# Loading the first-layer MLP weights in three DMAs of 112, 8 and 8 partitions instead of one of 128

## The chip, the cores and the metric

One core of one Trainium2 chip runs the whole program. The metric is device time in microseconds (us), lower is better. Executions of one kernel in one set of rounds agree within some 0.3%. Each kernel is compared with runs of the kernel before that were taken in the same rounds on the same chip.

## The reference, cut to what matters

A decode step of attention over a cached K and V, plus an MLP, added to a residual. The caches (8 x 32 heads x 4096 keys x 128, bf16, 268 MB each) are nearly all of the bytes. The MLP matters here only through its weights `w1`, 640 x 1728 bf16, 2.2 MB of 552 MB.

```python
xn = _layernorm(x)                                     # x: 8 x 1 x 640
out = x + attention(xn, k_cache, v_cache, wq, wo) + mlp(xn, w1, b1, w2, b2)
# mlp: h = gelu(layernorm(xn) @ w1 + b1);  h @ w2 + b2
```

## The kernel before: the parts that matter

All large loads go out from the sync engine (SP) on one DMA queue, in a fixed order: K tile 0, `wq`, K tile 1, `w1`, `w2` (two pieces), then V and K tiles in turn, 4 MB each, until the end. A tile's buffer is reused once it has been consumed; two K and two V buffers keep the queue filled.

```python
def ld(pos, dst, src, W, sem, R=()):          # a DMA from SP; W: what it writes, R: what it waits for
    add("sp", pos, lambda e: e.dma_start(dst, src() if callable(src) else src), R=R, W=W, sem=sem)
...
w1_sb = arena[:, o1:o2].rearrange("p (c f) -> p c f", c=DC)      # 128 partitions x 17280 bytes
...
ld(-95.2, w1_sb, B_w1.rearrange("(k c) f -> k c f", c=DC), ["w1"], "w1")
ld(-95.1, w2_sb[:, 0:FC, :], B_w2[0:FC * P, :].rearrange("(k c) n -> k c n", c=FC), ["w2"], "w2")
ld(-95.0, w2_sb[0:FR, FC, :], B_w2[FC * P:F, :], ["w2r"], "w2r")
...
add("pe", 1.0, pe_hidden, R=["w1", "xT1", "b1", "onesb", "zeros"], W=[it_h, "w1free"], X=[it_h])
```

Partition k of `w1_sb` gets five neighbouring rows of `w1`, one contiguous run of 17280 bytes. I call one partition's contiguous piece of a DMA a *run*; in the trace it is one DMA packet. Every load of 16 engines has added 16 to its semaphore, one step per engine, when all of them are done (W1: 16 steps, from 39.42 to 41.15 us). I call each of these steps a *landing*.

## Time and profile before

| | before |
|---|---|
| median, first set of runs | 1290.24 us (4 runs, 1289.99 to 1290.49) |
| profiled span | 1288.2 us |
| DMA rate over the span | 429 GB/s |
| VectorE busy | 1141.1 us, 89% |
| W1 runs (128 of 17280 bytes) | mean 0.648 us, median 0.644 |
| W2 runs (128 of 16640 bytes) | mean 0.628 us, median 0.620 |
| last K tile: mean / last of its 16 landings | 1252.46 / 1253.76 us |

The first fence has lines of the page of the kernel before: DMA busy share (in tenths) and GB/s in 40 slices of 32.2 us, then the load queue's packets, MB and share of 16 engines.

```profile
DMA  9999999999999999999999999999999999999998
GB/s 408 423 427 429 437 429 432 429 429 433 431 431 432 432 428 434 429 433 429 431 431 432 430 428 436 429 433 429 430 432 432 430 435 429 428 434 430 432 430 351
...
q1 hardware_dynamic: 21440, 551.80, 99.8%
```

Next, the chain of waits of the kernel before (start us, us, what). From 247 us until the short tail at the end it is only V-cache loads and the matmuls that consume them. With the queue at 99.8% throughout, what the DMA engines lose early can be expected to arrive at the end.

```profile
1.22 23.81 DMA KV_sb<-in_A_wq_dram
...
56.79 28.81 DMA KV_sb<-in_A_k_cache_dram
...
247.41 34.57 DMA KV_sb<-in_A_v_cache_dram
...
1228.27 35.19 DMA KV_sb<-in_A_v_cache_dram
1263.50 3.62 PE PV_ps L630 x32
1267.14 15.92 DMA KV_sb<-in_A_v_cache_dram
```

The third view is a table by stretch: start and end, length, each engine's busy us and instructions, granted clock, DMA share, GB/s. Most of W1 and all of W2 travel in these 13 us, at 421 and 415 GB/s.

```profile
core 0: us, PE busy (x) PEld busy (x) DVE busy (x) ACT busy (x) POOL busy (x), PEclk, DMA share, GB/s
35.00:41.00 6.00, 5.32 (x76) 4.34 (x77) 5.97 (x3) 3.96 (x8) 0.00 (x0) 1.00 0.99 421
41.00:48.00 7.00, 4.51 (x83) 3.96 (x82) 6.96 (x3) 5.84 (x11) 0.00 (x0) 0.69 1.03 415
```

### The profile page before, as it was taken

To read this page: it belongs to the slowest core of one execution; us is meant where nothing else is said; L and a number is where in the kernel's file an instruction comes from. 1 tells how busy PE (TensorE), PEld (TensorE's weight loads), DVE (VectorE), ACT (ScalarE), POOL (GpSimd) and SP (SyncE) were. 2 spreads that over 40 slices of the span, in tenths; PEclk is the share of its full clock that TensorE was granted. 3 is DMA by queue.
4 is the path that set the end of the run, shared out by engine and by line. 5 is a ranking of instruction groups with operands and counts; after the bars stand their busy time and mean duration, and the time that the engine had idled before them with its cause. 6 is when DMAs were issued, how large, how long until landed. Compare 5 with 4: busy or idle time off the path is not lost.

```text
span 1288.2 us, 19951 instructions
## 1 busy us (share of the span) xinstructions
PE 641.0 (50%) x7931; PEld 403.3 (31%) x7934; DVE 1141.1 (89%) x680; ACT 496.9 (39%) x1243; POOL 0.2 (0%) x4
## 2 busy tenths in 40 slices
PE   2754454444554455454455444544544554455456
PEld 1433233223333233232233232332332332333332
DVE  4989999998898898898988988988989989889895
ACT  1444344334344234343243342443432443433432
POOL 0000000000000000000000000000000000000000
PEclk9755555565555655656656556555565556655556
DMA  9999999999999999999999999999999999999998
GB/s 408 423 427 429 437 429 432 429 429 433 431 431 432 432 428 434 429 433 429 431 431 432 430 428 436 429 433 429 430 432 432 430 435 429 428 434 430 432 430 351
DMA packets 21488, 552.00 MB, mean 429 GB/s; under 512 B 2313, under 2 KB 2401, under 8 KB 4450
## 3 DMA queue, kind: packets, MB, share of 16 engines
q1 hardware_dynamic: 21440, 551.80, 99.8%
q8 instruction: 8, 0.13, 0.0%
q14 instruction: 6, 0.05, 0.0%
q10 hardware_dynamic: 34, 0.02, 0.0%
HBM read 551.80 MB, written 0.01 MB: 428 GB/s over the span
## 4 chain that ended last, share of the span: by engine, by line
DMA 77%; DVE 11%; PE 8%; issue 4%; ACT 0%; SPq 0%; DVEq 0%
DMA KV_sb<-in_A_v_cache_dram 73%; PE PV_ps L630 7%; DVE Y_sb L558 6%; DVE Y_sb L562 3%; DMA KV_sb<-in_A_k_cache_dram 2%; DVE S_sb L565 2%; DMA KV_sb<-in_A_wq_dram 2%; DVE oTn_sb L679 0%; DVE M_sb L577 0%; PE CH_ps L579 0%; SPq L372 0%; DVE rinv_sb L611 0%; PE PV_ps L640 0%; PE TR_ps L691 0%; PE TR_ps L470 0%
## 5 line engine op out<-in xcount | busy, mean ns | idle before, releaser
L558 DVE TENSOR_TENSOR Y_sb<-KV_sb,qbc_sb 128x6144 bf16<-128x6144 bf16 x128 | 429.0, 3352 | 67.0 <-DMA KV_sb<-in_A_k_cache_dram 51.8
L565 DVE TENSOR_REDUCE S_sb<-Y_sb 128x48 f32<-128x3072 bf16 x128 | 429.2, 3353 | 4.4
L529 ACT ACTIVATE KT_sb<-TR_ps 128x1024 bf16<-128x1024 bf16 x256 | 254.6, 1021 | 232.5 <-PE TR_ps L526 231.1
L630 PE MATMUL PV_ps<-KV_sb,P_sb 128*16 128x512 bf16 x2040 | 222.0, 609 | 132.0 <-DMA KV_sb<-in_A_v_cache_dram 132.0
L526 PE MATMUL TR_ps<-ident_bf,KV_sb 128*128 128x128 bf16 x2048 | 248.3, 308 | 53.1 <-DMA KV_sb<-in_A_k_cache_dram 52.6
L562 DVE TENSOR_TENSOR Y_sb<-Y_sb 128x3072 bf16<-128x3072 bf16 x128 | 225.0, 1758 | 4.4
L526 PEld LDWEIGHTS TR_ps<-ident_bf,KV_sb 128*128 128x128 bf16 x2048 | 200.4, 141 | 63.3 <-DMA KV_sb<-in_A_k_cache_dram 57.5
L536 PE MATMUL S_ps<-qk_sb,KT_sb 128*128 128x4 bf16 x2048 | 98.0, 170 | 140.3 <-ACT KT_sb L529 138.3
L649 ACT ACTIVATE E_sb<-PV_ps 128x512 bf16<-128x512 f32 (+1 forms) x65 | 38.5, 592 | 308.2 <-PE PV_ps L630 306.2
L536 PEld LDWEIGHTS S_ps<-qk_sb,KT_sb 128*128 128x128 bf16 x2048 | 85.9, 109 | 171.7 <-ACT KT_sb L529 171.7
L630 PEld LDWEIGHTS PV_ps<-KV_sb,P_sb 128*16 128x16 bf16 x2040 | 60.7, 120 | 246.3 <-DMA KV_sb<-in_A_v_cache_dram 137.2
L597 ACT ACTIVATE P_sb<-S_sb,NB_sb 32x128 bf16<-32x128 f32 x256 | 101.9, 398 | 3.8
L655 PE MATMUL C_ps<-sel_bf,E_sb 128*128 128x4 bf16 x256 | 16.9, 172 | 159.7 <-DVE rinv_sb L611 133.7
L591 ACT ACTIVATE NB_sb<-CH_ps 128x2 f32<-128x2 f32 (+1 forms) x33 | 5.7, 172 | 177.1 <-PE CH_ps L587 177.1
L579 PE MATMUL CH_ps<-ident_f,M_sb 128*2 128x128 f32 (+1 forms) x33 | 12.2, 369 | 117.7 <-DVE M_sb L577 117.7
L655 PEld LDWEIGHTS C_ps<-sel_bf,E_sb 128*128 128x128 bf16 x256 | 11.4, 103 | 189.4 <-DVE rinv_sb L611 136.4
L546 ACT ACTIVATE S_sb<-S_ps 32x32 f32<-32x32 f32 x256 | 48.2, 188 | 32.0 <-PE S_ps L536 29.8
L597 ACT ACTIVATION_READ_ACCUMULATOR P_sb<-S_sb,NB_sb 32x1 f32 x256 | 47.1, 184 | 0.0
L579 PEld LDWEIGHTS CH_ps<-ident_f,M_sb 128*2 128x2 f32 (+1 forms) x33 | 2.6, 80 | 120.6 <-DVE M_sb L577 120.6
L673 DVE MEMSET oTn_sb<- 128x16 uint32 x30 | 2.2, 72 | 31.1 <-PE ACC_ps L704 31.1
L581 DVE TENSOR_REDUCE M_sb<-CH_ps 2x4 f32<-2x128 f32 (+1 forms) x33 | 9.2, 279 | 15.9 <-PE CH_ps L579 15.9
L704 PE MATMUL ACC_ps<-oTn_sb,wo_sb 128*128 128x8 bf16 x600 | 20.8, 169 | 0.0
(96 smaller groups left out, 212.8 us busy)
## 6 DMA issues: line engine op xcount, KB each, us to landing
KV_sb<-in_A_k_cache_dram SPq DMA_DIRECT2D x64, 4096.0 KB, 26.8
KV_sb<-in_A_v_cache_dram SPq DMA_DIRECT2D x63, 4096.0 KB, 35.2
KV_sb<-in_A_wq_dram SPq DMA_DIRECT2D x1, 5120.0 KB, 23.8
wo_sb<-in_A_wo_dram SPq DMA_DIRECT2D x7, 640.0 KB, 30.8
KV_sb<-in_B_w_dram SPq DMA_DIRECT2D x1, 2160.0 KB, 39.0
w_sb<-in_B_w_dram SPq DMA_DIRECT2D x1, 2080.0 KB, 43.8
KV_sb<-in_A_v_cache_dram SPq DMA_DIRECT2D x1, 2048.0 KB, 12.7
KV_sb<-in_A_v_cache_dram SPq DMA_DIRECT2D x2, 1024.0 KB, 15.1
```

What stands on the lines that cost most here:

```text
L526: r = e.transpose(TR_ps[:, it.box[0], jj * P:(jj + 1) * P], kv[:, n * BK + jj, :], ident_bf[:, :])
L529: add("act", t - 0.59 + 0.12 * n, lambda e: e.activation(KT_sb[:, m % NS, :, :].rearrange("p a b -> p (a b)"), TR_ps[:, it.box[0], :], ACT ...
L536: r = e.matmul(S_ps[:, c:c + HT], KT_sb[:, m % NS, jj, :], qk_sb[:, :, i], start=True, stop=True)
L546: r = e.activation(S_sb[s, g % SR, i, 0:JP], S_ps[s, 0:JP * HT].rearrange("p (j a) -> p j a", a=HT)[:, :, a], ACT.Copy)
L558: return e.tensor_tensor(y, kv[:, j0:j1, :], qbc_sb[:, g % 2, i, :][:, None, :].to_broadcast([P, nj, P]), ALU.mult)
L562: lambda e, y=y, y2=y2: e.tensor_tensor(y2, y[:, :, 0:P // 2], y[:, :, P // 2:P], ALU.add),
L565: lambda e, y2=y2, j0=j0, j1=j1: e.tensor_reduce(S_sb[:, g % SR, i, j0:j1], y2, AX.X, ALU.add),
L597: r = e.activation(P_sb[s, i, :, a, :], S_sb[s, g % SR, i, :].rearrange("p (m c) -> p m c", c=4), ACT.Exp, bias=NB_sb[s, g % 2, i:i + 1], ...
L630: r = e.matmul(PV_ps[32 * ct:32 * ct + HT * 4, t % 2, :], P_sb[:, i, m, :, :].rearrange("p a c -> p (a c)"), vv[:, 4 * m:4 * m + 4, :, :], ...
L649: add("act", pos, lambda e: e.activation(E_sb[:, k, 0:n], PV_ps[:, k, 0:n], ACT.Copy), R=[("PV", k)] + ["wo"] * (t % GT and not last), W=[ ...
L655: r = e.matmul(OT_i, E_sb[:, t % 2, c * P:(c + 1) * P], sel_bf[:, c:HT * 4:4], start=(c == 0), stop=(c == 3 and not last))
L704: r = e.matmul(ACC_ps[:, c * B:(c + 1) * B], wo_sb[:, a, c * P:(c + 1) * P], oTn_sb[:, a, :], start=False, stop=False, skip_group_check=True)
```

## The change

The intent: both DMAs of 8 partitions go to the same eight of the 16 DMA engines, which I call the *first eight* (no trace numbers the engines). With 112 + 8 + 8 partitions, the first eight move 7 + 1 + 1 = 9 runs of W1 and the other eight move 7. If the first eight were ahead of the others, the field (how far the sixteen engines lie apart in time) would be evened out.

```diff
-        ld(-95.2, w1_sb, B_w1.rearrange("(k c) f -> k c f", c=DC), ["w1"], "w1")
+        w1v = B_w1.rearrange("(k c) f -> k c f", c=DC)
+        for n, (p0, p1) in enumerate(((0, P - 16), (P - 16, P - 8), (P - 8, P))):
+            ld(-95.2 + 0.01 * n, w1_sb[p0:p1], w1v[p0:p1], ["w1_%d" % n], "w1")
...
-        add("pe", 1.0, pe_hidden, R=["w1", "xT1", "b1", "onesb", "zeros"], W=[it_h, "w1free"], X=[it_h])
+        add("pe", 1.0, pe_hidden, R=["w1_0", "w1_1", "w1_2", "xT1", "b1", "onesb", "zeros"], W=[it_h, "w1free"], X=[it_h])
```

## The prediction

> **What bounds the kernel.** The DMA engines. The page's DMA row is 9 in 39 of 40 slices; the queue table gives the load queue 99.8% of 16 engines' span. In the trace's DMA packets a 32768-byte run takes 1.213 us on an engine and the next starts within some 5 ns. The chain of waits from 247 us to the end is only V-cache loads and their matmuls. So the time is nearly the longest sum of packets on one engine.
>
> **How the engines stand.** A load adds 16 to its semaphore, one per engine, so the landings show the engines' lags. The first K tile lands within 0.46 us; the tile landing at 1251 us has seven engines within 0.5 us, one 1.0 us and eight 1.7 to 2.5 us behind. The jumps (1.55 or 0.7 to 1.0 us, one engine each) coincide with 16 KB and 8 KB packets of the instruction queues. The eight-row bias load at 6 us lets me mark eight engines; following them by phase, I find late engines in both halves. So I don't believe that the first eight have time to spare.
>
> **The change.** Bytes stay. [...] The trace agrees for the eight-row loads: eight data packets, nine semaphore steps. So 112 rows give each engine seven, and each eight-row piece gives one to engines 0 to 7. A 17280-byte run takes 0.644 us: engines 0 to 7 do 9 instead of 8 (+0.64 us), the others 7 (-0.64 us). Two more issues (0.45 us each) are hidden behind queued loads. W1 is first used at 48.7 us and has landed by 41.2 us, so no compute wait changes.
>
> With equal speed, one of the first eight that is already 2.4 us late gets 0.64 us more: end +0.3 to +0.6 us.
>
> **What I think is added.** [...] The queue is never empty, so lost engine time is not regained: all of it is critical.
>
> **Time.** 1290.2 + 0.5 if ports don't collide (1 in 4), +3 to +7 us if they do. I say 1294.5 us, 1290.1 to 1298.0 in 8 of 10. Faster by over 2%: 0.005; within 2%: 0.985; slower: 0.01.
>
> **What would show it.** [...] Spread of the 16 landings of the first V tile: from 1.7 us to 6 us (ports), or 2 to 3 us (none). The 19.4 us between V landings unchanged.
>
> **What would make it wrong.** The late engines being the last eight (then -0.5 us); instruction fetches moving to other engines; buffers that hide the collision.

Its sum came to +3 to +7 us if engines get in each other's way when they write (its word is "ports"; no run shows ports), to +0.5 us if not (1 in 4), and the point was 1294.5 us. Nothing shown here gave the +3 to +7, or the 6 us of the landings' spread, its size. "Engines 0 to 7" are the first eight as defined above. The lags are rounded: the 16 landings of the tile at 1251.43 us lie 0 to 0.30 (seven), 0.89 (one) and 1.61 to 2.33 us (eight) behind the first. The jump of W1: beside the 16 KB instruction packet at 34.07 us (1.00 us long) one engine's part landed 1.26 us after the fifteenth (41.15 against 39.89).

## More of the kernel before

The issue table (KB each, us to landing) has W1 in one DMA of 2160 KB:

```profile
KV_sb<-in_B_w_dram SPq DMA_DIRECT2D x1, 2160.0 KB, 39.0
w_sb<-in_B_w_dram SPq DMA_DIRECT2D x1, 2080.0 KB, 43.8
```

## The result, and the profile after

The changed kernel takes 1297.3 us (median of 4, 1296.94 to 1298.4) against 1290.24 (4 runs): +7.1 us. The ratio is 1.0056, 95% interval 1.0039 to 1.0074. A ratio here is the mean time of one kernel's fast runs over that of the other's of the same rounds, so not quite the ratio of the quoted medians. By the 2% rule that is "same"; it is nevertheless clear of the noise.

The page after, same lines. The DMA row still says 9 in 39 of 40 slices. The second slice of GB/s fell from 423 to 337, and no other early slice fell like it:

```profile
DMA  9999999999999999999999999999999999999998
GB/s 406 337 434 425 436 431 430 433 428 434 430 431 434 427 435 430 430 435 427 434 431 430 434 428 434 431 430 434 427 435 430 430 435 427 435 429 430 435 430 342
...
q1 hardware_dynamic: 21456, 551.80, 99.7%
```

The chain after. The first K-tile wait is 35.44 us instead of 28.81 (+6.63). After that the waits are as long as before (35.17 us for 35.19) and everything is about 7 us later (1235.24 for 1228.27):

```profile
1.20 24.11 DMA KV_sb<-in_A_wq_dram
...
57.09 35.44 DMA KV_sb<-in_A_k_cache_dram
...
254.34 34.84 DMA KV_sb<-in_A_v_cache_dram
...
1235.24 35.17 DMA KV_sb<-in_A_v_cache_dram
1270.46 3.40 PE PV_ps L634 x31
1273.88 16.10 DMA KV_sb<-in_A_v_cache_dram
```

The same two stretches after: 287 and 191 GB/s, at a DMA share of 1.07 and 0.93. The engines are "busy" with packets that take longer:

```profile
35.00:41.00 6.00, 5.41 (x72) 4.40 (x71) 5.96 (x3) 3.95 (x9) 0.00 (x0) 1.00 1.07 287
41.00:48.00 7.00, 5.52 (x81) 4.78 (x80) 6.97 (x3) 5.84 (x12) 0.00 (x0) 1.00 0.93 191
```

The issue table shows the three pieces (no time to landing is given, since they have 16, 9 and 9 landings and not 16 each):

```profile
KV_sb<-in_B_w_dram SPq DMA_DIRECT2D x1, 1890.0 KB
KV_sb<-in_B_w_dram SPq DMA_DIRECT2D x2, 135.0 KB
w_sb<-in_B_w_dram SPq DMA_DIRECT2D x1, 2080.0 KB, 49.5
```

Now the packets of the trace, counted by size. "Extra" is the time over the full-rate duration of a run (0.644 us for W1, 0.620 us for W2), summed and divided by 16, so the mean loss of one engine. The 16 W1 packets that start last are taken as the small pieces; the trace doesn't name a packet's engine, so a few may be on the wrong side, which does not change the sum.

```
packets                                 before mean   after mean   after max   extra after, us per engine
W1, the 112 first (112-partition piece)     0.649        0.963       1.33        2.23
W1, the 16 last  (two 8-partition pieces)   0.644        2.039       2.47        1.40
W2, 128                                     0.628        0.960       2.45        2.72
```

The sum is 6.35 us; before it was 0.10. The landings agree. The 16 landings of the last K tile moved by +6.33 us in the mean (1252.46 to 1258.79) and +6.94 us at the last (1253.76 to 1260.70). So nine tenths of the delay is in the mean of all sixteen engines, and 0.61 us is a field spread a little wider. The profiled runs differ by 1296.94 - 1290.0 = 6.94 us.

And it was not the first eight alone: all 16 runs of W1 or W2 that started between 41.5 and 44 us took 2.29 to 2.47 us, whether they were W1 runs (7 of them) or W2 runs (9, of which at least seven follow seven W1 runs in the strings told of above, so they are on other engines than the small pieces).

### The profile page after: what moved, and what is told of

The parts are those of the page before. It is cut to its first block, busy times and chain, and to the rows that moved or that the text cites. A ratio compares the mean times of both kernels' runs of the same rounds, so it can differ in the third digit from the quotient of the medians.

```text
span 1295.2 us, 19956 instructions
## 1 busy us (share of the span) xinstructions
PE 642.7 (50%) x7934; PEld 405.1 (31%) x7934; DVE 1141.1 (88%) x680; ACT 497.3 (38%) x1243; POOL 0.2 (0%) x4
## 4 chain that ended last, share of the span: by engine, by line
DMA 77%; DVE 11%; PE 8%; issue 4%; ACT 0%; SPq 0%; DVEq 0%
DMA KV_sb<-in_A_v_cache_dram 73%; PE PV_ps L634 7%; DVE Y_sb L562 6%; DMA KV_sb<-in_A_k_cache_dram 3%; DVE Y_sb L566 3%; DVE S_sb L569 2%; DMA KV_sb<-in_A_wq_dram 2%; DVE oTn_sb L683 0%; DVE M_sb L581 0%; PE CH_ps L583 0%; SPq L372 0%; DVE rinv_sb L615 0%; PE PV_ps L644 0%; PE TR_ps L695 0%; PE TR_ps L474 0%
## 6 DMA issues: line engine op xcount, KB each, us to landing
KV_sb<-in_A_k_cache_dram SPq DMA_DIRECT2D x64, 4096.0 KB, 26.8
```

## The experiments

Three explanations were to be told apart.

- **Crowded destinations** ("Ports theory"). Each small DMA writes a few neighbouring partitions; the supposition is that engines which write neighbouring partitions at the same time slow each other. The changed kernel's 2.04 us a run for 0.644 is in keeping with it but doesn't single it out.
- **Uneven bytes.** The first eight engines move two runs more than the others.
- **The split itself, or the source.** More DMAs, a shared semaphore, small DMAs; or rows of W1 that lie close together in the memory.

All kernels are edits of the kernel before; the wait of `pe_hidden` names all pieces of W1. The cuts below show added lines only, some of them shortened: each kernel but the last puts these loads in place of the one DMA of W1. Each gave a result that passed the comparison. "Landing" is the mean / last of the 16 landings of the last K tile, in the profiled run.

### Equal counts, 112 and 16

```diff
+        w1p = [(slice(0, 112), slice(0, 112)), (slice(112, 128), slice(112, 128))]
+        for n, (d, s) in enumerate(w1p):
+            ld(-95.2 + 0.01 * n, w1_sb[d], w1v[s], ["w1_%d" % n], "w1")
```

> Pieces of 112 and 16 partitions: every engine again moves 8 runs, so nothing is uneven. Ports theory [...]: runs of the 112-row piece take about 1.0 us as in the changed kernel (+2 us), the 16-row piece [...] some 2.5 us a run instead of 0.64, and drags the W2 runs beside it; end 1294 to 1297 us. Uneven-bytes theory: 1290.2. Split theory (cost of more DMAs on one semaphore): at most half of the 7 us, below 1294.

1295.18 us against 1290.24 (ratio 1.0037, 1.0020 to 1.0053), landing 1258.18 / 1259.69. The 112-row runs took 1.04 us on average, the 16-row ones 1.68. Eight runs an engine if the 16 rows go to all of them (that each got one was not looked up), and +4.9 us: uneven bytes are not the cause of the bulk.

### Three DMAs cut along the free axis

```diff
+        w1f = w1_sb.rearrange("p c f -> p (c f)")
+        w1s = B_w1.rearrange("(k c) f -> k (c f)", c=DC)
+        w1p = [(0, 7560), (7560, 8100), (8100, 8640)]
+        for n, (c0, c1) in enumerate(w1p):
+            ld(-95.2 + 0.01 * n, w1f[:, c0:c1], w1s[:, c0:c1], ["w1_%d" % n], "w1")
```

> Three DMAs again, in the same proportions (7/8, 1/16, 1/16 of the bytes), but cut along the free axis: each still has 128 partitions and all 16 engines. Ports theory: runs at full rate (about 0.28 us for 15120 B cut would be wrong; 15120 B 0.56 us, 1080 B 0.05 us), end 1290.2 within 0.6. Uneven-bytes theory: 1290.2 too. Split theory: 1294 or more.

1290.64 us against 1290.24 (ratio 1.0004, 0.9988 to 1.0021), landing 1252.74 / 1253.93. The runs of 15120 bytes took 0.565 us (median), those of 1080 bytes 0.048. Three DMAs on one semaphore, and no difference that the runs can tell from zero: the split as such costs nothing that could be measured. The two stretches run at 421 and 424 GB/s:

```profile
35.00:41.00 6.00, 5.52 (x73) 4.46 (x74) 5.97 (x3) 3.90 (x9) 0.00 (x0) 1.00 1.01 421
41.00:48.00 7.00, 5.06 (x83) 4.33 (x84) 6.96 (x3) 5.96 (x11) 0.00 (x0) 1.00 1.07 424
```

### Blocks of eight partitions, and every fourth partition

Both kernels load partitions 32 to 127 in one DMA and 0 to 31 in four DMAs of eight. They differ in which eight:

```diff
 # block version
+        w1p = list(zip(*[[slice(32, 128)] + [slice(8 * i, 8 * i + 8) for i in range(4)]] * 2))
 # every-fourth version
+        w1p = list(zip(*[[slice(32, 128)] + [slice(i, i + 29, 4) for i in range(4)]] * 2))
```

> Partitions 32 to 127 in one DMA (6 runs an engine), then partitions 0 to 31 as four DMAs of 8 neighbouring partitions, so the first eight engines do 10 runs and the others 6. Ports theory: the four small pieces run at about 2.4 us a run, end 1298 to 1304 us. Uneven-bytes theory: two runs more than before on the first eight, 2 x 0.644 = +1.3 us at most, end 1291.5. Split theory: five DMAs instead of three, +14 us, 1304.

> As the block version, the same five DMAs and the same 10 and 6 runs, but each small piece takes every fourth partition of 0 to 31 (and the same rows of W1)[...]. Ports theory: the small pieces' runs at 0.64 to 0.8 us; what is left is the uneven count (+1.3) and the 96-row piece (+1 to +2): end 1291.5 to 1294. Uneven-bytes theory: 1291.5. Split theory: as the block version.

Block: 1299.96 us, +9.7 (ratio 1.0076, 1.0059 to 1.0093), landing 1260.83 / 1264.03. Every fourth: 1295.43 us, +5.2 (ratio 1.0039, 1.0022 to 1.0056), landing 1256.55 / 1258.93. The small pieces' runs took 1.73 us (median) as blocks and 0.67 us spread out. (I had expected 2.4 us for the blocks, and 2.5 us for the 16-row piece above, which took 1.68: too much both times; the changed kernel had shown 2.29 to 2.47 us between 41.5 and 44 us.) The number of DMAs, their size and the number of packets are the same (21472 on the load queue in both). The two stretches, block version first:

```profile
35.00:41.00 6.00, 5.30 (x71) 4.34 (x71) 5.97 (x3) 3.95 (x10) 0.00 (x0) 1.00 1.02 228
41.00:48.00 7.00, 4.55 (x80) 4.00 (x80) 6.96 (x3) 5.99 (x12) 0.00 (x0) 0.71 1.08 174
```

```profile
35.00:41.00 6.00, 5.46 (x71) 4.40 (x71) 5.97 (x3) 3.92 (x9) 0.00 (x0) 1.00 1.01 228
41.00:48.00 7.00, 5.42 (x80) 4.77 (x80) 6.96 (x3) 5.88 (x11) 0.00 (x0) 1.00 0.99 373
```

In the first stretch both move the 96-partition piece, at 228 GB/s; in the second come the small pieces, 174 against 373 GB/s. I had put the every-fourth version at 1294 at most, 1.4 us too low, because the 96-row piece is dearer than I had thought: its runs took 1.17 to 1.18 us on average, 6 x 0.53 = 3.2 us per engine. Why the 112- and 96-row pieces are slow was not tested alone, and no run shows how their rows are dealt out to the engines.

### Destination or source

The two preceding kernels change the destination partitions and the rows read together. These two change one of them. Their W1 rows land on the wrong partitions, so they compute something else. (The comparison doesn't see an error of this size in the MLP.)

```diff
+        C = [slice(32, 128)] + [slice(8 * i, 8 * i + 8) for i in range(4)]
+        S = [slice(32, 128)] + [slice(i, i + 29, 4) for i in range(4)]
 # (written out in the kernels)
+        w1p = list(zip(S, C))      # destination spread, source in blocks
+        w1p = list(zip(C, S))      # destination in blocks, source spread
```

> WRONG RESULT ON PURPOSE. Five DMAs as in the block and the every-fourth version; here the four small pieces write every fourth partition of 0 to 31 but read eight neighbouring rows of W1, so only the destination is spread. Ports theory: as the every-fourth version, small runs 0.65 us, end 1294.5 to 1296.5. Source theory (rows that lie close together in the memory are slow to read): as the block version, small runs 1.7 us, end 1298.5 to 1302.5.

> WRONG RESULT ON PURPOSE. The reverse: the four small pieces read every fourth row of W1 but write eight neighbouring partitions, so only the source is spread. Ports theory: as the block version, small runs 1.7 us, end 1298.5 to 1302.5. Source theory: as the every-fourth version, 0.65 us, end 1294.5 to 1296.5.

Destination spread: 1295.12 us against 1290.33, landing 1256.26 / 1258.39, small runs 0.69 us (median). Source spread: 1300.31 us, landing 1261.78 / 1264.29, small runs 2.03 us. The destination partitions decide; spreading the source saves nothing. That the small runs took 2.03 us here and 1.73 us in the block version, with the same destinations, is a difference between two profiled runs: the times of the two kernels (1298.78 to 1301.22 and 1298.68 to 1302.53 us) do not differ. The eight engines were nearer in step here (the last eight small runs started within 1.07 us of each other, in the block version within 1.51 us), which may be the reason; that was not tested. The second stretch of each, destination spread first:

```profile
41.00:48.00 7.00, 5.43 (x81) 4.78 (x80) 6.97 (x3) 5.84 (x12) 0.00 (x0) 1.00 0.99 382
```

```profile
41.00:48.00 7.00, 5.21 (x79) 4.57 (x76) 6.96 (x3) 5.89 (x11) 0.00 (x0) 1.00 0.99 133
```

### Half as spread: every second partition

```diff
+        w1p = [slice(32, 128)] + [slice(16 * (i // 2) + i % 2, 16 * (i // 2) + i % 2 + 15, 2) for i in range(4)]   # both sides
```

> The same five DMAs, each small piece on every second partition of 16[...]. Ports theory: in between[...], small runs 1.0 to 1.3 us, end 1296.5 to 1299. Theory that any stride cures it: as the every-fourth version, 0.65 us and 1295.4.

1298.2 us against 1290.33, +7.9, landing 1258.58 / 1261.50, small runs 1.23 us (median). So with the eight partitions of a small piece 4, 2 and 1 apart the runs took 0.67, 1.23 and 1.73 us. Not every stride cures it; the time falls as the partitions lie further apart.

### Spread, but at the upper end

```diff
+        w1p = [slice(0, 96)] + [slice(96 + i, 96 + i + 29, 4) for i in range(4)]     # both sides
```

> The every-fourth version moved to the upper end: partitions 0 to 95 in one DMA, then every fourth partition of 96 to 127. [...] Ports theory: [...] small runs 1.0 to 1.3 us instead of 0.67, W2 runs slowed too; end 1296.5 to 1299.5. If only the spread inside the piece counts: as the every-fourth version, 0.67 us and 1295.4.

1298.05 us against 1290.56, +7.5, landing 1259.25 / 1262.86, small runs 1.33 us (median) instead of 0.67. Inside a piece the partitions are four apart, as at the lower end, where the runs were at nearly full rate. So the spread inside a piece is not enough; where the piece lies counts too. I had expected it from which partitions the other engines write with W2 meanwhile; the trace does not tell which those are, so the cause is not shown.

### Two halves

```diff
+        w1p = [(slice(0, 64), slice(0, 64)), (slice(64, 128), slice(64, 128))]
```

> Two DMAs of 64 partitions, all 16 engines on each, four runs an engine in each, nothing uneven and no small DMA. Ports theory: [...] every run takes 2 x 0.644 = 1.29 us and all engines lose 8 x 0.645 = 5.2 us; end 1294.5 to 1296.5. Any theory that blames unevenness, small DMAs or eight-row shapes: 1290.3.

1296.08 us against 1290.56 (ratio 1.0045, 1.0028 to 1.0061), landing 1258.24 / 1259.56. Runs took 1.35 us (median), 17280 / 1.35 = 12.8 GB/s an engine where one DMA of 128 partitions gave 17280 / 0.644 = 26.8. This is the plainest case: all engines (each half has 16 landings), no small DMA, runs at half rate. (The factor of two was assumed beforehand; no run shows how the rows are dealt out, nor why it is two.) The first stretch has 219 GB/s for the 421 before:

```profile
35.00:41.00 6.00, 5.52 (x74) 4.46 (x75) 5.96 (x3) 3.90 (x9) 0.00 (x0) 1.00 1.04 219
```

### Blocks of four partitions

```diff
+        w1p = [slice(32, 128)] + [slice(4 * i, 4 * i + 4) for i in range(8)]     # both sides
```

> Partitions 32 to 127 in one DMA, then 0 to 31 as eight DMAs of four neighbouring partitions: [...] so the first four engines do 14 runs, the other twelve 6. Ports theory: [...] small runs 1.7 to 2.5 us, the first four engines end late; end +12 to +22 us, 1302 to 1312. [...] if engines that write elsewhere are slowed too (as they were in the block version), the twelve others' W2 runs beside the small pieces take far over 0.62 us[...].

1306.36 us against 1290.56 (2 runs), +15.8, landing 1264.73 / 1269.18. The small runs took 1.53 us on average, 1.96 at most. All 73 W2 runs that started on other engines between 42 and 50 us took 1.0 us or more, against 0.62. So engines that have no part in the small pieces are slowed beside them. This is how the loss in the changed kernel could fall on all sixteen. By what path it reaches them is open.

Not all of the +15.8 us is runs that took longer, though: W1 landed only at 55.88 us here, its matmuls waited 7.2 us for it, and between 92 and 95 us the DMA queue stood partly empty, which costs 0.9 us per engine. In the changed kernel and the block version the queue had no such gap.

### The uneven count alone

First try: 7/8 of each run in one DMA of 128 partitions, the last 1/8 (2160 bytes) by the first eight engines alone, in 16 DMAs of every fourth partition of a quarter.

```diff
+        w1p = [(slice(0, P), 0, 7560)] + [(slice(32 * a + i, 32 * a + i + 29, 4), 7560, 8640)
+                                          for a in range(4) for i in range(4)]
```

> The uneven count alone: the first 7/8 of every run goes in one DMA of 128 partitions; the last 1/8 (2160 B a row) goes in 16 DMAs of 8 partitions four apart, all on the first eight engines[...]. So the first eight engines move what nine runs are and the others seven, as in the change[...]. Ports theory: 15120 B runs 0.565 us, 2160 B runs about 0.09 us, all at full rate; end 1290.3 to 1291.3 (+0.3 to +0.6 for the uneven count and some 0.2 for the small packets). If unevenness were the cause of the +7 us: 1296 or more. If the change's intent was right (the first eight have time to spare): below 1290.

1292.57 us against 1290.33, +2.2 (ratio 1.0015, 0.9998 to 1.0032), landing 1253.84 / 1255.88: above my range. It is not clean, since half of the pieces write partitions 64 to 127, where spread pieces were slow in the run at the upper end (1.33 us), and the W2 runs beside them took 0.74 us on average. So a second try leaves W1 as it was and adds two runs' worth to the first eight, on every fourth partition of 0 to 31 (0.67 us a run above), into a tile that nobody reads:

```diff
+        pad_sb = sb("pad_sb", [P, 4320], BF)
+        for n in range(4):
+            ld(-95.19 + 0.001 * n, pad_sb[n:n + 29:4, :], w1s[n:n + 29:4, 0:4320], ["pad%d" % n], "pad")
```

> The kernel before, W1 in one DMA, plus four more DMAs of 8 partitions four apart in 0 to 31 (8640 B a run, rows of W1 again, into a tile that nobody reads): the first eight engines get two runs' worth more (2 x 0.644 = 1.3 us), the others nothing[...]. Theory that engines near the end of the field are in both halves: the end moves by all of it, +1.1 to +1.4, 1291.5. Theory behind the change, the first eight have time to spare: the late ones of the field are the last eight, 2.3 us behind, so the first eight can take 1.3 us more and the end stays at 1290.3 to 1290.6. [...]

1291.73 us against 1290.40 (5 runs, ratio 1.0013, 1.0000 to 1.0027), landing 1253.28 / 1255.20. The interval just touches 1, but the lowest of the five runs (1291.46) lies above the highest of the nine of the kernel before (1290.82). The extra runs took 0.326 us each, full rate, and the W2 runs 0.645 on average although the first eight were now behind: engines out of step hardly disturbed each other here. The time moved by 1.3 us, as much as two runs take (4 x 0.326). The last landing moved by 1.44. So among the first eight there are engines that have no time to spare, and the premise of the change did not hold in these runs.

No variant beat the kernel before.

## Why the prediction was right, point by point

The time, 1297.3 us, lies in the range (1290.1 to 1298.0) and 2.8 us above the point. The +7.1 us are at the very top of the +3 to +7 us that the prediction gave for colliding writers, and 0.7 us more would have left the range: that the destination would slow the small pieces was right in kind, and that the number held was in part luck, since its parts were wrong and their size was not shown.

- *The DMA engines bound the kernel and lost time is not regained.* Right: +6.63 us in the chain's first K-tile wait, waits of equal length afterwards, +7 us at the end.
- *Each engine's count 9 or 7; the issue of two more DMAs hidden; W1 in time for its matmuls.* Right, though W1 was in time by little: it had landed by 47.75 us, and the first of its matmuls ran at 49.20 us, 48.66 before.
- *Uneven count +0.3 to +0.6 us, engines near the end of the field are in both halves.* In keeping with it: the last landing moved 0.61 us more than the mean, though the slow writes may have part in that. That the first eight have no slack was tested by the extra loads (+1.3 us).
- *Colliding writes are the main term.* Right in kind: destination spread or not, 0.69 against 2.03 us a run; the source made no such difference. The eight-row packets took 2.04 us on average, 2.47 at most, less than the mark that the prediction had set for them.
- *Its size was the sum of wrong parts.* The terms had too much for the small runs, too little for the 112-row piece, and nothing on the other engines' W2 runs. Measured: small runs 2.0 us on average, 2.5 at most (extra of 1.40 us over 16 engines, so 2.8 us on each of the eight); the 112-row piece +2.23 us; and +2.65 us in the W2 runs (0.960 against 0.628 us, 128 of them over 16 engines), which I had left at full rate. With the uneven 0.61 us that makes 6.9 us. The overestimate of one part and the two underestimates nearly cancelled, which is luck.
- *Spread of the landings 6 us.* Wrong: the first V tile's 16 landings spread over 2.98 us (1.67 before), because the loss fell on all engines. The step of the prediction that failed is the one that gave the delay to the eight writers alone.

What stays open: why writes to neighbouring partitions, and to fewer than 128, are slow; how they slow engines that have no part in them; how the 112 and 96 rows are dealt out; and why spread pieces were slower at the upper end. In the block version the eight engines were not in step (their last small runs started over 1.51 us), so how many wrote at once was not measured.

## What to carry to other kernels

As far as these runs show, a DMA-bound kernel does best to keep all 128 partitions in each DMA (W1 runs of 0.644 us, for 0.96 with 112 partitions, 1.17 with 96 and 1.35 with 64); to cut a load, cut the free axis (three DMAs cost nothing that could be measured, two of 64 partitions cost 5.5 us for 2.2 MB). Before moving work between DMA engines, find out from the 16 landings and by an extra load whether those engines really have time to spare. And judge DMA by GB/s: the busy row stayed at 9 while the rate of one stretch halved (415 to 191 GB/s).
